# G's mixes by accumulating DMAs, w_out's mixes on VectorE, six batches' state products from one split of w_in, and the state read's scalings on ScalarE

## The chip, the cores and the metric

One core of a Trainium2 chip runs the whole program. The metric is device time in microseconds (us), the median of several executions; lower is better. Engines are named as in the profile: PE (TensorE), PEld (its weight loads), DVE (VectorE), ACT (ScalarE), POOL (GpSimd) and SP (SyncE, which issues most DMAs).

## What is computed

Attention between 512 tokens and 32 state rows per head, in both directions, and on its result a two-layer network with `h - tanh(h)` in the middle:

```python
scores = scale * np.matmul(x, state.transpose(0, 1, 3, 2))      # softmax over the 32 state rows
xread = np.matmul(a, state)
scores2 = scale * np.matmul(state, x.transpose(0, 1, 3, 2))     # softmax over the 512 tokens
sread = np.matmul(a2, x)
...
h = x @ w_in            # x: 4608 rows of 512 (8 batches of 512 + 32); w_in 512 x 2048
g = h - np.tanh(h)
return (g @ w_out)      # w_out 2048 x 512
```

## The kernel before

The 4096 token rows are eight chunks of 512, one for each batch; the 256 rows of the state read are a ninth, chunk 8. Since `xread` is `a @ state`, the kernel never forms it: for each batch it computes m = state x w_in (256 rows by 2048) and then h = a x m, in 16 *hidden tiles* of 128 columns (`Chunk.hidden`, L405 to L407; `finish` takes tanh on ACT and the difference on DVE, L419 and L421).

**Split products.** Each float32 operand is split into a high and a low part in the float32r format (`split`, L99: a cast on ACT, then a subtraction on DVE), and a product is three matmuls: high by high, high by low, low by high.

**Stage one** makes the chunks 0 and 1, while the weights come in as 64-bit words and are converted. w_in is kept in DRAM (`wf`), m of the batches 0 and 1 comes from whole-float32 matmuls (L165). m of the other six comes from generators, `m_units(g)`, of 16 units each, which split a piece of w_in (`wst`), multiply it by the state with 64-row matmuls (L198), copy out on ACT (L202), and store to DRAM (`mdram`, L205). g = 0 serves the batches 2 to 5. g = 1 serves 6 and 7: it reads and splits w_in a second time, has the state's high and low part side by side in one stationary operand, and leaves two addends, which `load_m` sums on DVE (L218). w_out's rows go to DRAM as high and low parts (`keep_row`, into `wod`), and `mix_rows` makes from each two rows four sums and differences of w_out's blocks (L718 to L723, on POOL), splits them and stores them in `wsd`.

**The pairs.** The chunks 2 to 7 are done as three pairs (`Pair`; the profile's W0m.., W1m.. and W2m.. tiles). With w_out in four blocks, a pair's product is made from seven block products instead of eight, m1 to m7 in the code, in the order of `ORDER`; some take mixes of the two chunks' g, some mixes of w_out. Each has four steps of twelve matmuls (L861), each step with a W tile of 512 KB loaded by SP (L807) into one of four `parts` buffers. The g of a pair stay whole in SBUF (`G`, in groups j = 0 to 3 of even and odd tiles, 128x1024 each). Mixes of G are made in place: two when four hidden tiles of the second chunk are done (`hidden_done`, L841), one ahead of each m5 split (L828), one behind each m6 split (L834), all on POOL but for six on DVE. A m5 product's operand is then split (`Pair.split`), and so on. While a pair runs its later products, the next chunk's hidden tiles stand between them. Chunk 8 comes last, with w_out's rows loaded back (`load_rows`).

**What sets the order.** A list of ticks, "P" for a product step and "H" for a hidden tile, is written out for each pair; tables (`ASIDE`, `KEEP`, `MIX`, `SIDES`) say at which step or tick a side unit (attention of a later batch, m units, rows kept, mixes) is handed over; the framework's scheduler then places instructions on each engine, which issues its own in that order. Pool sizes (`parts` 4, `twins` 2, two PSUM banks each in `ps_a` and `ps_h`) set when buffers come free.

**State read.** `state_read` divides by the softmax's sum with 64 scalings of 32x64 on DVE (L365).

Of the kernel before, what the change touches and what calls it, by code (L numbers as in the profile page):

```python
# [34 lines left out]
def attention_ffn(ctx: ExitStack, tc: tile.TileContext, xT, xn, bd, bh, sp, sm, sl, win, wout, xout, tout, sout):  # L35
# [133 lines left out]
    def m_units(g):  # L169

        raw = pool.tile([P, H, P], F32, tag="stage", name=f"smr{g}", bufs=SB)
        s = pool.tile([P, 2, H, P], F32R, tag="sm", name=f"sms{g}", bufs=1)
        if g == 0:
            nc.sync.dma_start(raw, sm)
            split(s[:, 0], s[:, 1], raw)
        else:
            nc.sync.dma_start(raw[:, :, 0:64], sl)  # L180
            split(s[:, 0, :, 0:64], s[:, 0, :, 64:128], raw[:, :, 0:64])
        for q in range(NQ):
            for k in range(2):
                w = pool.tile([P, 2, 512], F32, tag="wf", name=f"w1{g}{q}{k}", bufs=WB)
                nc.sync.dma_start(w, wf[q][:, 2 * k : 2 * k + 2])
                for c in range(2):
                    p = 2 * k + c

# [2 lines left out]
                    hs = slice(2 * c, 2 * c + 2)
                    stage = pool.tile([P, 2, 512], F32, tag="stage", name=f"st{g}{q}{p}", bufs=SB)
                    pss = [bank(ps_a, f"mps{g}{q}{2 * p + e}") for e in range(2)]
                    terms = [(0, 0), (0, 1)] + [(1, 0)] * (g == 0)
                    for n, (x, y) in enumerate(terms):
                        for e in range(2):
                            rows = slice(64 * e, 64 * e + 64)
                            nc.tensor.matmul(  # L198
                                pss[e], s[rows, x, 2 * p + e], t[rows, y], start=(n == 0), stop=(n == len(terms) - 1)
                            )  # L200
                    for e in range(2):
                        nc.scalar.copy(stage[:, e], pss[e])  # L202
                    for j in range(4):
                        dst = mdram[2 + j][q][0] if g == 0 else mdram[6 + j % 2][q][j // 2]
                        nc.sync.dma_start(dst[k, hs].rearrange("h n f -> n h f"), stage[32 * j : 32 * j + 32])  # L205
# [812 lines left out]
```

## Time and profile before

| | |
|---|---|
| median of 3 runs | 731.44 us (731.35 to 731.79) |
| the profiled execution | 733.29 us, its span 731.3 us |
| mean granted PE clock | 0.969 |
| busy PE, DVE, ACT, POOL | 670.3, 565.5, 399.3, 183.1 us |
| DMA | 164.29 MB, 225 GB/s on average |

The span reaches from the first to the last instruction of the profiled execution. Busy time of PE contains waits in its pipeline and slow clock, so that 92% is not all work. Rows of groups show line, engine, operation and tiles, then busy time and mean ns of one, then the idle time ahead of them and what ended it. In lists by time the first number is the start, the second the length.

### The profile page before, as it was taken

Reading aid. Unit: us, or ns where it says so; the run is one execution under the profiler, and the core shown is the slowest. Engines: PE = TensorE matmul, PEld = TensorE weight load, DVE = VectorE, ACT = ScalarE, POOL = GpSimd, SP = SyncE. Lnnn points to the kernel's source line nnn. Section 1 sums busy time; section 2 is a strip of 40 time slices with the busy share of each in tenths; the row PEclk is TensorE's granted clock in tenths of the full one; section 3 lists DMA queues with packets and bytes.
Section 4 is the critical chain, followed back from the end, with each engine's and each line's share of the span. In section 5 each row is a group of like instructions: output and inputs, shape, how many; then the busy total and the mean of one; then the engine's idle time right before and its main releaser. Section 6 shows DMA issues by size and latency. Waiting matters only on the chain.

```text
span 731.3 us, 9639 instructions
## 1 busy us (share of the span) xinstructions
PE 670.3 (92%) x3378; PEld 497.3 (68%) x3378; DVE 565.5 (77%) x781; ACT 399.3 (55%) x643; POOL 183.1 (25%) x99
## 2 busy tenths in 40 slices
PE   4899879999989798778999999788999999799997
PEld 2456657777766574556767777566788877587896
DVE  5899999769745979996669669997797698945442
ACT  3789757657545654535656666334654553343432
POOL 2000034755500025722000006563000069600000
PEclk9899999999999999998999999989999999999999
DMA  9799926986897545654788887647676644599600
GB/s 314 238 386 371 357 91 219 326 289 208 250 320 201 193 141 176 202 155 155 223 260 252 282 249 243 232 134 242 186 230 194 201 129 141 162 390 378 212 23 30
DMA packets 82672, 164.29 MB, mean 225 GB/s; under 512 B 8000, under 2 KB 40000, under 8 KB 82624
## 3 DMA queue, kind: packets, MB, share of 16 engines
q1 hardware_dynamic: 82624, 163.67, 67.5%
q8 instruction: 27, 0.44, 0.2%
q14 instruction: 21, 0.17, 0.1%
HBM read 116.98 MB, written 46.66 MB: 224 GB/s over the span
## 4 chain that ended last, share of the span: by engine, by line
PE 54%; DVE 28%; DMA 7%; issue 6%; ACT 2%; POOL 2%; SPq 0%; ACTq 0%; DVEq 0%; POOLq 0%
PE X L861 15%; PE hps L405 5%; PE hps L406 5%; PE hps L407 5%; PE Y0m L861 4%; DVE m L99 4%; PE mps L198 3%; PE Y1m L861 3%; PE ops L452 3%; PE ops L453 3%; PE ops L454 3%; DVE G L419 2%; PE Y2m L861 2%; POOL G L841 2%; DVE wst L99 1%
## 5 line engine op out<-in xcount | busy, mean ns | idle before, releaser
L841 POOL TENSOR_TENSOR G<-G,G 128x1024 f32<-128x1024 f32 x18 | 53.8, 2987 | 287.6 <-DVE G L419 286.9
L405 PE MATMUL hps<-aT,m 128*128 128x512 f32 x248 | 103.3, 417 | 18.4 <-DVE G L419 13.3
L406 PE MATMUL hps<-aT,m 128*128 128x512 f32 x248 | 99.7, 402 | 0.0
L407 PE MATMUL hps<-aT,m 128*128 128x512 f32 x248 | 99.4, 403 | 0.0
L419 DVE TENSOR_TENSOR G<-hps,t 128x512 f32<-128x512 f32 x96 | 64.9, 683 | 33.0 <-ACT t L419 32.7
L419 ACT ACTIVATE t<-hps 128x512 f32<-128x512 f32 x96 | 56.9, 597 | 57.1 <-PE hps L407 57.0
L405 PEld LDWEIGHTS hps<-aT,m 128*128 128x128 f32 x248 | 48.0, 194 | 41.9 <-DVE G L419 17.5
L99 DVE TENSOR_TENSOR g2m<-G,g2m 128x1024 fp32r<-128x1024 f32 x28 | 45.6, 1636 | 20.1 <-PE Y2m L861 7.8
L861 PE MATMUL X<-g0m,W0m 128*128 128x512 f32 x192 | 53.2, 421 | 6.5 <-ACT g0m L99 4.2
L407 PEld LDWEIGHTS hps<-aT,m 128*128 128x128 f32 x248 | 48.0, 194 | 12.0 <-issue 1.5
L406 PEld LDWEIGHTS hps<-aT,m 128*128 128x128 f32 x248 | 48.3, 195 | 11.0 <-issue 1.9
L453 PE MATMUL ops<-wo,g 128*128 128x512 f32 x128 | 51.3, 405 | 4.0 <-DVE wo L99 4.0
L718 POOL TENSOR_TENSOR wa<-wo 128x512 f32<-128x512 f32 x16 | 24.6, 1559 | 118.1 <-ACT wo11r L131 78.8
L99 ACT CAST g2m<-G 128x1024 fp32r<-128x1024 f32 x28 | 29.2, 1053 | 44.9 <-PE X L861 17.4
L99 DVE TENSOR_TENSOR m<-mr,m 128x1024 fp32r<-128x1024 f32 x31 | 51.2, 1653 | 1.3 <-ACT m L99 1.1
L861 PE MATMUL X<-g1m,W1m 128*128 128x512 f32 x192 | 50.0, 406 | 2.1 <-DVE g1m L99 2.1
L202 ACT COPY st<-mps 128x512 f32<-128x512 f32 x64 | 35.9, 589 | 29.3 <-PE mps L198 26.1
L861 PE MATMUL X<-g2m,W2m 128*128 128x512 f32 x192 | 47.1, 401 | 4.9 <-ACT g2m L99 2.8
L861 PEld LDWEIGHTS X<-g0m,W0m 128*128 128x128 f32 x192 | 37.2, 201 | 18.9 <-ACT g0m L99 4.8
L454 PE MATMUL ops<-wo,g 128*128 128x512 f32 x128 | 49.9, 395 | 0.0
L99 DVE TENSOR_TENSOR g1m<-G,g1m 128x1024 fp32r<-128x1024 f32 x28 | 39.5, 1416 | 12.4 <-PE X L861 7.3
L99 DVE TENSOR_TENSOR g0m<-G,g0m 128x1024 fp32r<-128x1024 f32 x28 | 38.2, 1366 | 12.2 <-ACT g0m L99 9.2
(265 smaller groups left out, 1465.8 us busy)
## 6 DMA issues: line engine op xcount, KB each, us to landing
md<-st SPq DMA_DIRECT2D x128, 128.0 KB, 2.6
mr<-md SPq DMA_DIRECT2D x24, 512.0 KB, 4.4
xT<-in_xT SPq DMA_DIRECT2D x16, 512.0 KB, 4.9
wod<-wo SPq DMA_DIRECT2D x16, 512.0 KB, 4.8
w<-wf SPq DMA_DIRECT2D x16, 512.0 KB, 4.4
wsd<-ws SPq DMA_DIRECT2D x16, 512.0 KB, 4.6
xn<-in_xn SPq DMA_DIRECT2D x16, 512.0 KB, 5.0
W0m<-wsd SPq DMA_DIRECT2D x16, 512.0 KB, 4.3
```

What stands on the lines that cost most here:

```text
L99: return nc.scalar.copy(hi, src), (sub or nc.vector).tensor_sub(lo, src, hi)
L198: nc.tensor.matmul(pss[e], s[rows, x, 2 * p + e], t[rows, y], start=(n == 0), stop=(n == len(terms) - 1))
L202: nc.scalar.copy(stage[:, e], pss[e])
L405: nc.tensor.matmul(ps, mhi[k][:, cols], ahi[:, k], start=(k == 0), stop=False)
L406: nc.tensor.matmul(ps, mhi[k][:, cols], alo[:, k], start=False, stop=False)
L407: made = nc.tensor.matmul(ps, mlo[k][:, cols], ahi[:, k], start=False, stop=(k == nk - 1))
L419: main(nc.scalar.activation(t, ps, AF.Tanh), nc.vector.tensor_sub(g, ps, t))
L453: nc.tensor.matmul(o, g[:, 0, tok], w[:, 1], start=False, stop=False)
L454: return nc.tensor.matmul(o, g[:, 1, tok], w[:, 0], start=False, stop=(f == NFF - 1)).ins
L718: nc.gpsimd.tensor_add(a[:, e].rearrange("p h n -> p (h n)"), w[:, 0], w[:, 1])
L841: main(eng.tensor_sub(c, d, c), eng.tensor_add(a, a, c))
L861: made = nc.tensor.matmul(out[t], w[:, e, x, cols], y[:, e], start=first and j == 0 and e == 0 and c == 0, stop=last and j == 3 and e == 1 ...
```

## The change

Four edits, and the tables that go with them.

1. G's mixes: `hidden_done` and both mixes in `split` become DMAs issued from POOL's queue that add their source onto their destination in SBUF (512 KB each, 48 in all). Since such a DMA only adds, half of the hidden tiles are stored with the other sign (t - h), m4's w_out block is stored negated, and some closing sums become differences. m5's mix now follows its split and m5 goes ahead of m6: m5 splits a, then a += d, then m6 splits a, then it is added onto m4's operand.
2. w_out's mixes: each converted row is also stored whole (`wfd`), `mix_rows` loads two rows from there, and makes the sums on DVE. m4's block, negated, is split and stored as a fifth row of `wsd`. `wod` is laid out by halves, so a row is stored and loaded back in two DMAs, and a pair's W tile is one run in a partition.
3. `m_units` has one generator: its 16 units serve all six batches. The batches 6 and 7 get 48 whole 128-row matmuls (one PSUM bank of `ps_h` a unit, `mls`) with a block-diagonal state operand, and one addend. The second pass (`m1` in the tables, 64 half-height matmuls, in the first two pairs) is gone, with its reads and splits of w_in and the sum in `load_m`.
4. The state read's 64 scalings are ACT activations with a scale.

```diff
-        "m0": [15, 16, 17, 17, 18, 19, 19, 20, 21, 21, 22, 23, 24, 25, 26, 27],
+        "m0": [14, 14, 15, 15, 16, 16, 17, 17, 18, 18, 19, 20, 20, 21, 22, 23],
...
-    MIX = [17 + 2 * x for x in range(7)] + [30]
+    MIX = [16, 17, 18, 19, 20, 22, 24, 26]
...
-            "m1": list(range(24, 72, 4)),
...
-            "m1": [2, 5, 8, 11],
...
+                    ps2 = bank(ps_h, f"mls{q}{p}")
...
+                    for n, (x, y) in enumerate(((0, 0), (0, 1), (1, 0))):
+                        nc.tensor.matmul(ps2, s1[:, x, p], t[:, y], start=(n == 0), stop=(n == 2))
+                    late = pool.tile([P, 512], F32, tag="c2", name=f"sl{q}{p}", bufs=CSB)
+                    nc.scalar.copy(late, ps2)
...
+                    for e in range(2):
+                        for j in range(2):
+                            rows = slice(64 * e + 32 * j, 64 * e + 32 * j + 32)
+                            nc.sync.dma_start(mdram[6 + j][q][k, 2 * c + e], late[rows])
...
-                nc.vector.tensor_add(r, r, r2)
...
+        nc.sync.dma_start(wfd[:, f], w)
...
-                nc.vector.tensor_scalar_mul(
+                nc.scalar.activation(
...
-                main(nc.scalar.activation(t, ps, AF.Tanh), nc.vector.tensor_sub(g, ps, t))
+                main(nc.scalar.activation(t, ps, AF.Tanh))
+                main(nc.vector.tensor_sub(g, ps, t) if f % 2 == i % 2 else nc.vector.tensor_sub(g, t, ps))
...
-        nc.sync.dma_start(wod[:, f % 2, f // 2], wo[f].bitcast(F32))
+        for half in range(2):
+            cols = slice(256 * half, 256 * half + 256)
+            nc.sync.dma_start(wod[:, f % 2, half, f // 2], wo[f][:, :, cols].bitcast(F32))
...
-        for e in range(2):
-            w = wo[2 * j + e].bitcast(F32)
-            nc.gpsimd.tensor_add(a[:, e].rearrange("p h n -> p (h n)"), w[:, 0], w[:, 1])
+        nc.sync.dma_start(a, wfd[:, 2 * j : 2 * j + 2].rearrange("p e (h n) -> p e h n", h=2))
...
+        nc.scalar.mul(neg[:, 0], a22, -1.0)
+        nc.vector.scalar_tensor_tensor(neg[:, 1], a22, -1.0, neg[:, 0], ALU.mult, ALU.subtract)
+        nc.sync.dma_start(wsd[:, 4, j // 2, j % 2], neg.bitcast(F32))
+        nc.vector.tensor_add(a22, a21, a22)
+        nc.vector.tensor_sub(a21, a11, a21)
+        nc.vector.tensor_sub(a11, a22, a11)
+        nc.vector.tensor_sub(a12, a11, a12)
...
-        ORDER = ("m1", "m2", "m6", "m5", "m7", "m3", "m4")
+        ORDER = ("m1", "m2", "m5", "m6", "m7", "m3", "m4")
...
-            if k == "m5":
-                main(nc.gpsimd.tensor_sub(src, self.source("m3", j), src))
...
+            if k == "m5":
+                main(self.add(src, self.source("m3", j)))
             if k == "m6":
-                b = self.source("m4", j)
-                main(nc.gpsimd.tensor_sub(b, b, src))
+                main(self.add(self.source("m4", j), src))
+
+        def add(self, dst, src):
+            return nc.gpsimd.dma_start(dst, src, accum_op=ALU.add)
...
-                eng = nc.vector if j == 3 else nc.gpsimd
-                main(eng.tensor_sub(c, d, c), eng.tensor_add(a, a, c))
+                main(self.add(a, c), self.add(c, d))
```

The instructions move with it. First PE in the first pair, before: `hps3_6` is a hidden tile of chunk 3, `mps100` an output of the second m pass, `sps41` scores of batch 4.

```order
L277 MATMUL sps41_2554<-xT40_2475,bdr4_2473 32x512 x2
L277 MATMUL sps41_2554<-xT41_2477,bdr4_2473 32x512 x2
L198 MATMUL mps100_2582<-wst100_2578,sms1_2572 128x512 x2
L405 MATMUL hps3_6_2626<-aT3_1840,m31_2491 128x512
L406 MATMUL hps3_6_2626<-aT3_1840,m31_2491 128x512
```

Now no such group stands in any pair. PE in stage one has the third output instead; these are the rows of one unit now (`mps20`, `mps21` the 64-row matmuls, `mls20` the whole ones), between a hidden tile of chunk 1 and its output product.

```order
L405 MATMUL hps1_4_1423<-aT1_517,m11_1420 128x512
L192 MATMUL mps20_1441<-wst20_1438,sms_1036 128x512
L192 MATMUL mps21_1442<-wst20_1438,sms_1036 128x512
L194 MATMUL mls20_1443<-wst20_1438,sls_1041 128x512
L192 MATMUL mps20_1441<-wst20_1438,sms_1036 128x512
L192 MATMUL mps21_1442<-wst20_1438,sms_1036 128x512
L192 MATMUL mps20_1441<-wst20_1438,sms_1036 128x512
L192 MATMUL mps21_1442<-wst20_1438,sms_1036 128x512
L194 MATMUL mls20_1443<-wst20_1438,sls_1041 128x512 x2
L451 MATMUL ops1_0_1303<-wo4_481,g1_4_1433 128x512
```

Each of the 16 units has gained three whole matmuls, and all of them now stand ahead of the first pair's first product; before, the last four 64-row outputs (12 matmuls) stood behind it. Last, POOL's queue in the third pair before: `G6` is the first chunk's g, `G7` the second's, the number behind them the first tile of the group.

```order
L841 TENSOR_TENSOR G7_4_5308<-G7_5_5319,G7_4_5308 128x1024 [waits DVE_49]
L841 TENSOR_TENSOR G6_4_4738<-G6_4_4738,G7_4_5308 128x1024 [waits Pool_49]
L834 TENSOR_TENSOR G6_5_4767<-G6_5_4767,G6_4_4738 128x1024 [waits Activation_49,Pool_49]
L828 TENSOR_TENSOR G6_0_4584<-G7_1_5231,G6_0_4584 128x1024 [waits DVE_49,Activation_49]
L841 TENSOR_TENSOR G7_8_5417<-G7_9_5428,G7_8_5417 128x1024 [waits DVE_49]
L841 TENSOR_TENSOR G6_8_4884<-G6_8_4884,G7_8_5417 128x1024 [waits Pool_49]
```

And now, with the semaphores that each waits for (DMASW are those of POOL's own DMAs):

```order
L838 DMA G6_0_4518<-G7_1_5153 128x1024 [waits DVE_49,Activation_49]
L838 DMA G6_8_4812<-G7_8_5333 128x1024 [waits DMASW7_49,DMASW5_49,DVE_49]
L838 DMA G6_1_4548<-G6_0_4518 128x1024 [waits DMASW4_49]
L838 DMA G7_8_5333<-G7_9_5344 128x1024 [waits DMASW5_49,DVE_49]
L838 DMA G6_4_4669<-G7_5_5238 128x1024 [waits DVE_49,Activation_49]
L838 DMA G6_8_4812<-G7_9_5344 128x1024 [waits DMASW1_49,DVE_49,Activation_49]
L838 DMA G6_12_5015<-G7_12_5418 128x1024 [waits DVE_49]
```

Each mix has become one DMA row; several wait for an earlier one's landing, and the group 12's first DMA stands behind the group 8's last.

More of the change, by code (lines that the diff above doesn't have):

```diff
@@ L187, in m_units @@
                     p = 2 * k + c
-                    t = twins(f"wst{g}{q}{p}", [P, 2, 512], F32R)
+                    t = twins(f"wst{q}{p}", [P, 2, 512], F32R)
                     split(t[:, 0], t[:, 1], w[:, c])
[L191 to L195, printed above, removed]
+                    pss = [bank(ps_a, f"mps{q}{2 * p + e}") for e in range(2)]
+                    ps2 = bank(ps_h, f"mls{q}{p}")
+                    for n, (x, y) in enumerate(((0, 0), (0, 1), (1, 0))):
                         for e in range(2):
                             rows = slice(64 * e, 64 * e + 64)
-                            nc.tensor.matmul(
-                                pss[e], s[rows, x, 2 * p + e], t[rows, y], start=(n == 0), stop=(n == len(terms) - 1)
-                            )
+                            nc.tensor.matmul(pss[e], s0[rows, x, 2 * p + e], t[rows, y], start=(n == 0), stop=(n == 2))
+                    for n, (x, y) in enumerate(((0, 0), (0, 1), (1, 0))):
+                        nc.tensor.matmul(ps2, s1[:, x, p], t[:, y], start=(n == 0), stop=(n == 2))
+                    late = pool.tile([P, 512], F32, tag="c2", name=f"sl{q}{p}", bufs=CSB)
+                    nc.scalar.copy(late, ps2)
+                    stage = pool.tile([P, 2, 512], F32, tag="stage", name=f"st{q}{p}", bufs=SB)
                     for e in range(2):
@@ L651, in attention_ffn @@
     first = afters[FILL[3]]
-    m1 = [m_units(g) for g in range(2)]
+    m1 = m_units()
     atts = {}
@@ L803, in load @@
                 odd, half = self.PURE[k]
-                src = wod[:, odd, 2 * j : 2 * j + 2, :, 256 * half : 256 * half + 256]
+                src = wod[:, odd, half, 2 * j : 2 * j + 2]
             else:
@@ L895, in load_rows @@
         wo[f] = big(f"wl{f}", [P, 2, DM], F32R)
-        nc.sync.dma_start(wo[f].bitcast(F32), wod[:, f % 2, f // 2])
+        for half in range(2):
+            cols = slice(256 * half, 256 * half + 256)
+            nc.sync.dma_start(wo[f][:, :, cols].bitcast(F32), wod[:, f % 2, half, f // 2])
     def hidden(c, f, own=None):
```

69 lines of the change are left out of this document (34 added, 35 removed).

## Prediction

> **What bounds the kernel now.** First the page, for the engines as a whole; then a table of engine busy time by stretch, to find where TensorE is not full.
>
> ```profile
> span 731.3 us, 9639 instructions
> PE 670.3 (92%) x3378; PEld 497.3 (68%) x3378; DVE 565.5 (77%) x781; ACT 399.3 (55%) x643; POOL 183.1 (25%) x99
> ...
> PE   4899879999989798778999999788999999799997
> ...
> POOL 2000034755500025722000006563000069600000
> PEclk9899999999999999998999999989999999999999
> DMA  9799926986897545654788887647676644599600
> ...
> PE 54%; DVE 28%; DMA 7%; issue 6%; ACT 2%; POOL 2%; SPq 0%; ACTq 0%; DVEq 0%; POOLq 0%
> ```
>
> PE is 92% busy, but its dips (slices 14 to 18, 25, 26 and 34) mostly sit where POOL is busy, and DVE holds 28% of the chain that ended last. So I cut the span at the first product of each of the three pairs (219.9, 423.0, 574.2) and at the last chunk (682.3).
>
> ```profile
> 0.00:219.91 219.91, 196.44 (x875) 135.63 (x875) 184.05 (x289) 143.25 (x249) 62.87 (x57) 0.98 0.82 280
> 219.91:423.00 203.09, 184.50 (x1025) 130.13 (x1025) 158.47 (x234) 113.76 (x181) 37.72 (x14) 0.96 0.65 203
> 423.00:574.20 151.20, 142.07 (x753) 108.12 (x752) 127.17 (x158) 77.12 (x113) 40.23 (x14) 0.95 0.67 216
> 574.20:682.30 108.10, 102.01 (x441) 82.59 (x441) 77.01 (x62) 46.34 (x59) 42.24 (x14) 0.98 0.69 242
> 682.30:731.30 49.00, 45.25 (x289) 40.81 (x287) 18.78 (x39) 18.82 (x44) 0.00 (x0) 0.98 0.17 56
> ```
>
> Columns: length, then PE, weight load, DVE, ACT and POOL busy, granted clock, DMA share, GB/s. Within the pairs, stretches without and with POOL work differ:
>
> ```profile
> 350.00:423.00 73.00, 73.00 (x433) 52.10 (x433) 51.21 (x89) 45.81 (x73) 0.00 (x0) 1.00 0.80 251
> 250.00:350.00 100.00, 82.86 (x435) 57.83 (x434) 86.26 (x108) 51.42 (x82) 37.72 (x14) 0.91 0.52 164
> 450.00:500.00 50.00, 40.87 (x217) 30.25 (x216) 49.45 (x54) 21.77 (x33) 27.86 (x11) 0.90 0.65 219
> 600.00:650.00 50.00, 45.01 (x189) 36.19 (x188) 39.91 (x28) 20.14 (x26) 33.33 (x11) 0.97 0.59 194
> ```
>
> Without POOL work PE is full at clock 1.00; with it, PE idles 17.1, 9.1 and 5.0 us and its clock falls as well. The reason is in DVE's own rows, grouped for 260 to 350 us (the first three lines) and for 350 to 410 us (the last two):
>
> ```profile
> L99 DVE TENSOR_TENSOR g0m<-G,g0m 128x1024 fp32r<-128x1024 f32 x12 | 18.6, 1558 | 6.0 <-ACT g0m L99 3.0 <-PE Y0m L861 1.5 <-issue 1.4
> L99 DVE TENSOR_TENSOR m<-mr,m 128x1024 fp32r<-128x1024 f32 x4 | 9.6, 2402 | 0.0
> L841 POOL TENSOR_TENSOR G<-G,G 128x1024 f32<-128x1024 f32 x6 | 16.8, 2793 | 86.0 <-DVE G L419 85.7
> ...
> L99 DVE TENSOR_TENSOR g0m<-G,g0m 128x1024 fp32r<-128x1024 f32 x11 | 13.4, 1221 | 5.1 <-ACT g0m L99 5.1
> L99 DVE TENSOR_TENSOR m<-mr,m 128x1024 fp32r<-128x1024 f32 x3 | 3.6, 1216 | 0.0
> ```
>
> The same subtraction takes 1.22 us alone and 1.56 to 2.40 us on average beside POOL's mixes: the two engines hold each other up, DVE falls behind, PE waits for it.
>
> **The change, part by part.** Names: a and c are the even tiles of a pair's first and second chunk, d the second's odd ones, with a number for the group of four.
>
> *G's mixes.* All 42 GpSimd subtractions and 6 on DVE become 48 accumulating DMAs, so DVE's operations go back to 1.22 us. The PE time to be had is idle time plus slow clock: 17.1 + (1 - 0.91) x 82.9 = 24.6 us in the first pair, 9.1 + 4.1 = 13.2 in the second, 5.0 + 1.4 = 6.4 in the third. If every operand then stood ready it would all come back. Against that stands the landing time t of an accumulating DMA, of which this trace has no row. The nearest are plain 512 KB DMAs:
>
> ```profile
> W0m<-wsd SPq DMA_DIRECT2D x16, 512.0 KB, 4.3
> W2m<-wsd SPq DMA_DIRECT2D x16, 512.0 KB, 5.0
> wo0d<-in_wout SPq DMA_DIRECT2D x1, 512.0 KB, 9.4
> 36.00:82.00 46.00, 44.38 (x174) 28.80 (x172) 44.35 (x80) 38.88 (x67) 0.00 (x0) 1.00 1.00 372
> ```
>
> Bounds: 4.3 us (a quiet queue) and 9.4 us (the slowest in the trace, in the start's saturated stretch). I take 6.5: the third pair's 5.0 plus a second 512 KB read at the 372 GB/s of a full stretch, 1.4 us. The Trainium skill bears on that second read: "Collectives: The Full Stack", Part 3, says that an add in the DMA path needs two source reads and so gets half a copy's rate. No run shows it yet; by a rate of half, 512 KB count as 1 MB.
>
> Four rows more, for what stands around such a DMA:
>
> ```profile
> L419 ACT ACTIVATE t<-hps 128x512 f32<-128x512 f32 x96 | 56.9, 597 | 57.1 <-PE hps L407 57.0
> L419 DVE TENSOR_TENSOR G<-hps,t 128x512 f32<-128x512 f32 x96 | 64.9, 683 | 33.0 <-ACT t L419 32.7
> L99 ACT CAST g2m<-G 128x1024 fp32r<-128x1024 f32 x28 | 29.2, 1053 | 44.9 <-PE X L861 17.4 <-PE Y2m L861 12.4 <-DVE G L841 8.3
> 522.93 2.72 PE X L861 x12
> ```
>
> What t costs: in the third pair the fourth m5 product is due 19.0 us after hidden tile 7_11 (five products of twelve matmuls, 2.72 us each, and four hidden tiles of six, 1.36). Its DMA (a12 += c12) can't be issued before tile 7_14 is through tanh and subtraction (0.60 + 0.68), 10.8 us after 7_11, and its operand then still has to be split, 2.3 us (ACT 1.05, DVE 1.22). Done at 10.8 + t + 2.3, it is late by t - 5.9. GpSimd's queue adds to it: a8 += c8, issued near 7_11, must land before a8's split, and the DMA a8 += d8, which waits for that split, stands ahead of a12's; above t = 8.5 the delay is therefore 2t + 4.6 - 19.0. Fourth m6 then needs t + 2.3 within four products, another t - 8.6. At 6.5 that is 0.6 us per pair. I keep 5, 4 and 3.4 us for this and for waits that stood behind the old ones: gains 20, 9 and 3.
>
> *w_in from one split.* PE's prices:
>
> ```profile
> 228.90 0.95 PE L198 MATMUL mps<-wst,sms 64*128 64x512 f32 x3
> 229.79 0.50 PE L405 MATMUL hps<-aT,m 128*128 128x512 f32 x1
> ...
> 290.05 0.73 PE L198 MATMUL mps<-wst,sms 64*128 64x512 f32 x2
> ...
> 290.71 0.50 PE L407 MATMUL hps<-aT,m 128*128 128x512 f32 x1
> ```
>
> A whole matmul costs 0.227 us (2.72 / 12), a lone group of two half-height ones 0.66 from start to start, of three 0.89. The 16 m1 units leave the pairs, about 1.2 us each: 12 in the first pair (14 us), 4 in the second (5). The last 12 half-height matmuls of m0, now before the first product instead of behind it, move 4 us from the first pair to stage one. Stage one also takes 48 new whole matmuls, 10.9 us, and about 1 us of extra switches: +16 there, -18 in the first pair, -5 in the second. Is stage one PE-bound where they land?
>
> ```profile
> 140.00:200.00 60.00, 60.00 (x285) 44.92 (x283) 46.85 (x66) 38.19 (x67) 34.74 (x30) 1.00 0.81 253
> ```
>
> PE is full from 140 to 200, so nothing hides them: the 16 us count whole. The floor would be nothing, if they filled the 23 us (219.9 - 196.4) that PE idles in stage one; but none of those lie here, where most of m0 falls.
>
> *DMA in stage one.*
>
> ```profile
> 197.97 6.99 DMA wsd<-ws
> ...
> 206.50 6.69 DMA out_x<-ob
> ...
> 422.44 0.43 SPq L205 DMA_DIRECT2D md<-st  x1
> ```
>
> New there: 16 w_out rows stored (4.2 MB), 8 loads of them (4.2), 8 negated blocks (2.1), 64 copies of late blocks (4.2): 14.7 MB. The share is 0.82 already (row above), at 280 GB/s; at 372 GB/s, 14.7 MB is 40 us of full load, and the room is 0.18 x 219.9 = 40 us. Between nothing and 40 I take 8 us: the start is saturated (1.00 above), and the stretch before the first product already waits for a store of mixes and one of outputs (first two rows), but the extra is spread out. SP issues all of it in order, about 110 issues more at 0.43 us, 47 us of SP's time in 220; a load of a w_out pair that waits for its buffer holds up m0's loads and stores and the first pair's weights behind it, and that is part of the 8.
>
> *Engines off the path.* Three rows price the rest.
>
> ```profile
> L365 DVE TENSOR_SCALAR sr<-rps,ri 32x64 f32<-32x64 f32 x64 | 18.0, 281 | 5.7 <-PE rps L359 4.7
> L218 DVE TENSOR_TENSOR mr<-mr,ml 128x1024 f32<-128x1024 f32 x8 | 15.9, 1992 | 4.1 <-DMA mr<-md 2.4 <-issue 1.0 <-DVE ri L342 0.7
> L99 DVE TENSOR_TENSOR wst<-w,wst 128x512 fp32r<-128x512 f32 x32 | 32.0, 1000 | 9.6 <-ACT wst L99 9.6
> ```
>
> DVE loses 18.0 + 15.9 + 16 us and gains 40 of 256 columns for w_out's mixes in stage one: between 0.28 us (64 columns, above) and 0.68 (512), say 0.4, 16 us; in return it no longer meets POOL's 62.9 us there. ACT takes the 64 scalings: from nothing more than DVE's 0.28 us each, 18 us, to twice that, on an engine that is idle 45% of the span; I count nothing. What hides them is that idle time; were it gone, tanh would come late and PE's hidden tiles with it. m0's third output takes the hidden tiles' two PSUM banks in turn; the first rival prices that.
>
> **Sum.** Stage one +16 + 8 = +24; first pair -20 - 18 = -38; second -9 - 5 = -14; third -3; last chunk 0. Total -31. Against the profiled run: its span 731.3 becomes 700.3, and 733.29 becomes 702.3. That run lies 1.85 us above the median of 731.44, so the median is forecast at 700.4, rounded 700.
>
> **Rivals.** *Stage one fills up.* All 40 us of new DMA load land on the path there instead of 8, or tanh waits for PSUM banks that m0's third output now shares. For it: share 0.82 to 1.00 above. Against: 100 us of it are PE-bound with DMA at 0.81. With 20 to 28 us more the time is 720 to 728. Chance 0.15.
>
> *Accumulating DMAs become the bound* (the other side). If t is long, each pair stalls at its fourth m5 and fourth m6 product by the two terms above: at 9.4 us 4.4 + 0.8 = 5.2 per pair, 16 in all, 714; at 11.5 us 8.6 + 2.9, 34 in all, and the gain is gone; at 15 us 15.6 + 6.4, 66 in all, 764. For it: pairs already run DMA at 0.65 to 0.69, and 48 DMAs add 25 MB of writes and up to 50 of reads against 17 MB taken away. Against: no 512 KB DMA of this trace lands later than 9.4. It decides at about 11.5 us. Chance 0.10.
>
> *The hold-up stays.* GpSimd still makes those DMAs' descriptors, and if DVE is held up by that as by the mixes, only the moved work is left: +24 - 18 - 5 = 732. For it: DVE slows beside every POOL mix seen here. Against: so far POOL read and wrote whole operands. Chance 0.05. The Trainium skill, "SBUF — State Buffer", section "Who interferes with whom", speaks against it: two-input subtractions would not meet descriptor writing; nothing here shows that.
>
> *Cover holds in stage one.* If DMA costs nothing, and part of the waits at 198 and 206 goes as m0 and the mixes now end earlier, stage one grows by 12 or so: 688. Chance 0.15.
>
> **How the numbers follow.** The forecast has 0.55; its own range, with stage one's DMA from 0 to 16 and t from 4.3 to 9.4, is 690 to 722. Rivals reach 682 below (688 with 6 us more from the kept waits) and 728 above; what lies outside is the third rival, most of the second and the forecast's tails, under 0.2. 0.2% of the time, 1.5 us, is about what a measurement of this kernel tells from no change. Faster: 0.55 + 0.15 + 0.15, less 0.01 for t near the deciding point: 0.84. Same: 0.03, slower: 0.13, shared between the second and third rivals and that 0.01.
>
> **What would show it.** Right: DVE's 128x1024 splits near 1.22 us throughout the pairs; no PE dip at 250 to 350; first product near 244 us; first pair near 165 us, second 137, third 105. Wrong: splits still at 1.6 or more, accumulating DMAs landing after 9 us, waits of g0m on them, or a first product past 255.

## The result, and the profile after

The changed kernel takes 755.87 us (median of 4 runs, 752.84 to 758.45) beside 731.62 us (731.35 to 732.8): a ratio of 1.0327, 95% interval [1.0283, 1.0371]. It is slower, on the other side of the forecast and outside its range. The profiled execution of one run below, e1, was in a slower state (823.79 us at a mean clock of 0.75, beside 715.81 to 719.83 us for its other three), so that only its time is used. First the page of the changed kernel.

```profile
span 756.7 us, 9651 instructions
PE 679.7 (90%) x3362; PEld 505.4 (67%) x3362; DVE 462.1 (61%) x727; ACT 405.4 (54%) x683; POOL 45.6 (6%) x57
...
PE   5899889986899888986899999789999998588997
...
POOL 1000000000000000121100001220000012100000
PEclk9899999998699999999999999988999999799999
DMA  9799988898888845799977678999656799999610
...
PE 40%; DMA 13%; DVE 1%; issue 1%; ACT 1%; POOL 0%; ACTq 0%; DVEq 0%; SPq 0%; POOLq 0%
```

DVE is down by 103 us of busy time and POOL by 137, and DVE's share of the chain that ended last has gone from 28% to 1%. DMA stands there now with 13%. The DMA row has nines in the slices 18 to 20, 26 to 28 and 33 to 37; before, of these only 36 and 37 had them. Next, the table by stretch: columns as before, cut at the first product of each pair (263.8, 442.4, 586.1) and at the last chunk (707.6).

```profile
0.00:263.80 263.80, 231.13 (x950) 152.89 (x951) 190.18 (x336) 164.21 (x291) 3.74 (x9) 0.94 0.90 300
263.80:442.40 178.60, 162.47 (x982) 122.83 (x982) 110.09 (x168) 100.62 (x175) 14.04 (x16) 0.96 0.76 214
442.40:586.10 143.70, 135.40 (x706) 105.42 (x705) 88.73 (x126) 75.76 (x117) 13.89 (x16) 0.95 0.83 228
586.10:707.60 121.50, 105.44 (x442) 83.51 (x441) 54.27 (x58) 46.06 (x59) 13.91 (x16) 0.94 0.98 283
707.60:756.70 49.10, 45.21 (x289) 40.77 (x287) 18.78 (x39) 18.78 (x44) 0.00 (x0) 1.00 0.17 56
```

Stage one grew by 43.9 us. The first pair shrank by 24.5 and the second by 7.5, and the third, the shortest, grew by 13.4. Its DMA share is 0.98. Now the groups of the splits of the three pairs, and POOL's DMA issues.

```profile
L838 POOL DMA_DIRECT2D G<-G x48 | 41.8, 884 | 610.2 <-DVE ri L340 295.0 <-DVE G L418 107.6 <-DMA G<-G 76.8
...
L100 DVE TENSOR_TENSOR g0m<-G,g0m 128x1024 fp32r<-128x1024 f32 x28 | 34.0, 1221 | 23.7 <-ACT g0m L100 18.6 <-PE X L864 3.2 <-PE Y0m L864 1.8
L100 DVE TENSOR_TENSOR g1m<-G,g1m 128x1024 fp32r<-128x1024 f32 x28 | 33.9, 1220 | 20.1 <-ACT g1m L100 11.6 <-PE X L864 5.6 <-ACT s1m L880 2.1
L100 DVE TENSOR_TENSOR g2m<-G,g2m 128x1024 fp32r<-128x1024 f32 x28 | 33.9, 1223 | 45.2 <-ACT g2m L100 20.8 <-PE X L864 12.6 <-issue 5.7
```

The splits take 1.22 us in all three pairs: the hold-up of DVE is gone, as forecast, and descriptor writing on POOL does not bring it back. What came in its place is in the page's rows of DMAs (queue with packets, MB and its share of 16 engines; then KB each and median us to landing):

```profile
q0 software_dynamic: 6912, 25.17, 17.6%
...
G<-G POOLq DMA_DIRECT2D x48, 512.0 KB, 9.3
...
W2m<-wsd SPq DMA_DIRECT2D x20, 512.0 KB, 7.8
```

An accumulating DMA lands after 9.3 us, not 6.5, and 17.6% of 756.7 us is 133 us of all 16 engines for 48 of them, 2.77 us each. The third pair's weights land after 7.8 us, where they took 5.0. In the list of waits (total, times, longest) these stand:

```profile
POOL G L838 <- DMA G<-G: 76.8, 17, 11.2
...
ACT g2m L100 <- DMA G<-G: 20.4, 2, 13.8
...
ACT wn L719 <- DMA wa<-wfd: 18.4, 6, 5.7
ACT g1m L100 <- DMA G<-G: 16.5, 3, 7.4
```

The timeline of ACT and PE in the second pair shows how such a wait reaches PE (start, length, in brackets the idle time before and its releaser):

```profile
488.52 1.04 ACT L100 CAST g1m<-G 128x1024 fp32r<-128x1024 f32 x1 [7.39 <-DMA G<-G]
489.48 1.08 ACT L417 ACTIVATE t<-hps 128x512 f32<-128x512 f32 x2
...
490.84 0.80 PE L403 MATMUL hps<-aT,m 128*128 128x512 f32 x1 [4.61 <-DVE G L418]
```

ACT's cast waits 7.4 us for a landing, and two tanh stand behind it in ACT's queue. PE, whose hidden tile needs the PSUM bank that they free, idles 4.6 us, and the wait is put down to DVE's subtraction behind the tanh. In the third pair PE's longest wait, 7.9 us at the fourth m5 product, is for a cast that waits for the addition issued at 638.58. From there to 696.4 us the chain is mostly transfers: the five pieces below are 45.7 of these 57.8 us (first the row of waits, then start and length).

```profile
PE Y2m L864 <- ACT g2m L100: 7.9, 1, 7.9
...
638.58 11.29 DMA G<-G
...
653.36 10.37 DMA wl<-wod
663.80 9.82 DMA W2m<-wsd
676.50 7.00 DMA W2m<-wsd
689.11 7.25 DMA W2m<-wsd
```

Last, stage one. The stretch from 180 to 200 us, in which PE was full before, and two lines of it:

```profile
180.00:200.00 20.00, 12.76 (x36) 6.81 (x34) 14.28 (x28) 9.34 (x18) 0.00 (x0) 0.66 0.95 315
```

```profile
186.15 0.42 ACT L719 ACTIVATE wn<-wa 128x256 fp32r<-128x256 f32 x1 [5.66 <-DMA wa<-wfd]
...
187.12 0.79 PE L192 MATMUL mps<-wst,sms 64*128 64x512 f32 x2 [4.50 <-ACT wst L100]
```

ACT waits for a pair of w_out's rows, with the cast of w_in's piece behind it, and PE waits for that cast. The granted clock is 0.66 in this stretch.

### The profile page after: what moved, and what is told of

It reads as the page before. It is cut to its first block, busy times and chain, and to the rows that moved or that the text cites. A ratio compares the mean times of both kernels' runs of the same rounds, so it can differ in the third digit from the quotient of the medians.

```text
span 756.7 us, 9651 instructions
## 1 busy us (share of the span) xinstructions
PE 679.7 (90%) x3362; PEld 505.4 (67%) x3362; DVE 462.1 (61%) x727; ACT 405.4 (54%) x683; POOL 45.6 (6%) x57
## 3 DMA queue, kind: packets, MB, share of 16 engines
q0 software_dynamic: 6912, 25.17, 17.6%
## 4 chain that ended last, share of the span: by engine, by line
PE 40%; DMA 13%; DVE 1%; issue 1%; ACT 1%; POOL 0%; ACTq 0%; DVEq 0%; SPq 0%; POOLq 0%
PE X L864 14%; DMA G<-G 5%; PE hps L403 5%; PE hps L404 5%; PE hps L405 5%; DMA W2m<-wsd 3%; PE Y1m L864 3%; DMA W1m<-wsd 2%; PE Y2m L864 2%; PE Y0m L864 2%; DMA out_t<-ob0m 2%; DMA wl<-wod 1%; PE ops L452 1%; PE ops L451 1%; PE ops L453 1%
## 5 line engine op out<-in xcount | busy, mean ns | idle before, releaser
L838 POOL DMA_DIRECT2D G<-G x48 | 41.8, 884 | 610.2 <-DVE ri L340 295.0
L100 DVE TENSOR_TENSOR g2m<-G,g2m 128x1024 fp32r<-128x1024 f32 x28 | 33.9, 1223 | 45.2 <-ACT g2m L100 20.8
L418 DVE TENSOR_TENSOR G<-t,hps 128x512 f32<-128x512 f32 x48 | 32.7, 682 | 45.6 <-ACT t L417 45.6
L452 PE MATMUL ops<-wo,g 128*128 128x512 f32 x128 | 53.0, 414 | 3.1 <-DVE wo L100 3.0
L864 PE MATMUL X<-g0m,W0m 128*128 128x512 f32 x192 | 51.0, 407 | 4.6 <-DVE g0m L100 2.3
L418 DVE TENSOR_TENSOR G<-hps,t 128x512 f32<-128x512 f32 x48 | 33.0, 687 | 33.5 <-ACT t L417 33.2
L451 PE MATMUL ops<-wo,g 128*128 128x512 f32 x128 | 46.7, 421 | 5.4 <-ACT g L100 3.4
L100 ACT CAST g1m<-G 128x1024 fp32r<-128x1024 f32 x28 | 29.1, 1052 | 36.7 <-DMA G<-G 16.5
L100 DVE TENSOR_TENSOR g0m<-G,g0m 128x1024 fp32r<-128x1024 f32 x28 | 34.0, 1221 | 23.7 <-ACT g0m L100 18.6
L453 PE MATMUL ops<-wo,g 128*128 128x512 f32 x128 | 47.7, 405 | 0.0
L864 PE MATMUL X<-g1m,W1m 128*128 128x512 f32 x192 | 46.8, 391 | 1.0 <-DMA W1m<-wsd 1.0
L100 DVE TENSOR_TENSOR g1m<-G,g1m 128x1024 fp32r<-128x1024 f32 x28 | 33.9, 1220 | 20.1 <-ACT g1m L100 11.6
```

Source lines behind the costliest of these rows:

```text
L100: return nc.scalar.copy(hi, src), (sub or nc.vector).tensor_sub(lo, src, hi)
L418: main(nc.vector.tensor_sub(g, ps, t) if f % 2 == i % 2 else nc.vector.tensor_sub(g, t, ps))
L451: nc.tensor.matmul(o, g[:, 0, tok], w[:, 0], start=(f == 0), stop=False)
L452: nc.tensor.matmul(o, g[:, 0, tok], w[:, 1], start=False, stop=False)
L453: return nc.tensor.matmul(o, g[:, 1, tok], w[:, 0], start=False, stop=(f == NFF - 1)).ins
L838: return nc.gpsimd.dma_start(dst, src, accum_op=ALU.add)
```

## The experiments

Two questions: is the loss in the pairs that of the accumulating DMAs, and by what mechanism, and what fills stage one? The stretches of every run that is read below, in us from its timeline, cut at the first m0 matmul (m units of the batches 2 to 5) and then as above. Each row is one profiled execution, which lies up to 4.3 us from the run's median (f1 4.3 above it, e4 4.2 below), so a difference of a few us between two rows is not firm.

| run | to first m0 | to first product | pair 1 | pair 2 | pair 3 | median |
|---|---|---|---|---|---|---|
| before | 105.9 | 114.0 | 203.1 | 151.2 | 108.1 | 731.62 |
| after | 109.1 | 154.7 | 178.5 | 143.7 | 121.5 | 755.87 |
| e2_g_mixes_pool | 108.9 | 152.1 | 173.8 | 138.8 | 111.4 | 735.6 |
| e3_wout_resident | 101.6 | 154.1 | 177.2 | 142.7 | 120.4 | 745.81 |
| e4_both | 101.7 | 151.9 | 167.9 | 133.2 | 101.7 | 711.45 |
| e5_plain_copy | 109.4 | 151.8 | 171.8 | 129.6 | 105.8 | 716.43 |
| f1_two_pass_m | 104.7 | 128.3 | 182.1 | 142.3 | 101.8 | 705.56 |
| f2_m0_spread | 102.7 | 143.5 | 171.1 | 133.2 | 101.3 | 702.36 |
| f3_neg_buffer | 102.4 | 148.3 | 170.4 | 133.2 | 100.8 | 705.73 |
| g1_spread_and_buffer | 102.7 | 140.3 | 170.4 | 133.2 | 102.0 | 698.34 |
| g2_before_g_dve | 106.0 | 113.7 | 192.9 | 146.2 | 101.0 | 710.57 |
| g3_before_g_dve_one_split | 106.8 | 131.1 | 174.3 | 136.4 | 100.0 | 702.54 |
| g4_rows_late | 108.0 | 152.5 | 178.1 | 143.5 | 120.2 | 753.82 |
| h1_dma_where_slack | 104.3 | 138.2 | 165.1 | 132.7 | 107.4 | 698.92 |
| h3_dma_where_due | 101.7 | 140.0 | 172.4 | 135.3 | 110.9 | 710.63 |
| j1_dma_queue_order | 103.2 | 138.3 | 180.3 | 145.2 | 125.6 | 744.07 |
| j2_dma_all | 102.7 | 138.0 | 177.5 | 141.8 | 120.3 | 733.6 |

**e1, G's mixes on DVE.** The changed kernel with one line exchanged:

```diff
         def add(self, dst, src):
-            return nc.gpsimd.dma_start(dst, src, accum_op=ALU.add)
+            return nc.vector.tensor_add(dst, dst, src)
```

> The changed kernel with G's 48 mixes as additions on VectorE in place of accumulating DMAs; all else stays. Theory: the DMAs' landing (9.3 us, median) is what stalls the pairs and fills the DMA engines in the third; so the three pairs (178.6, 143.7, 121.5 us) fall to about 160, 135 and 106, stage one stays at 264, and the time is about 714. Rival 1 (VectorE becomes the bound: 48 additions of 1.26 us are 60 us more on an engine that also makes the splits): the pairs stay as they are or lengthen, 750 or more. Rival 2 (the loss is all in stage one, the pairs are held by something else): the time stays within 5 us of 756.

718.05 us, ratio to before 0.9808 [0.9774, 0.9841], near the 714 of its theory and 38 us less than the changed kernel. The accumulating DMAs alone turn a gain into a loss.

**e2, the same additions on POOL** (`nc.gpsimd.tensor_add(dst, dst, src)`).

> The changed kernel with G's 48 mixes as additions on GpSimd, as the kernel before had them, with the new order m5 ahead of m6. Theory: the hold-up between GpSimd and VectorE comes back, VectorE's 128x1024 splits beside it go from 1.22 us to 1.6 to 2.4, and the pairs take what they took before less the second m pass: about 183, 147 and 107 us; with stage one at 264 the time is about 750. Rival (the hold-up never cost much, the landing time of the DMAs is the whole loss): as with VectorE, about 714.

735.6, ratio 1.0059 [1.0038, 1.0081], lower than expected. The hold-up comes back, with the splits of the three pairs at 1.45, 1.66 and 1.74 us on average; but even so POOL is cheaper here than the DMAs, by 20 us, half of it in the third pair (111.4 beside 121.5).

**e3, w_out's sums made from the rows in SBUF**, without `wfd`.

```diff
-        nc.sync.dma_start(wfd[:, f], w)
...
-        nc.sync.dma_start(a, wfd[:, 2 * j : 2 * j + 2].rearrange("p e (h n) -> p e h n", h=2))
+        for e in range(2):
+            w = wo[2 * j + e].bitcast(F32)
+            nc.vector.tensor_add(a[:, e].rearrange("p h n -> p (h n)"), w[:, 0], w[:, 1])
```

> The changed kernel with the w_out mixes' inputs made on VectorE from the rows that are in SBUF (high plus low part), instead of being stored to DRAM and loaded back; no row is stored whole. Theory: ScalarE's wait for those loads (18.4 us in six waits, with the splits for m0 queued behind it) is what stage one loses beyond its new matmuls; stage one goes from 264 to about 245, the time to about 738. Rival (stage one is long because of the new matmuls and of DMA load as a whole, 0.90 share): it shortens by less than 6 us, since 8.4 of 79 MB go, and the time stays at 750 or above.

745.81, ratio 1.0192 [1.0169, 1.0215]. This lies between what its theory and its rival gave. In stage one the gain is all ahead of the first m0 matmul (109.1 to 101.6), where `wfd` was stored; from there to the first product nothing changed (154.7 and 154.1). Taking away ACT's wait for these loads, which the timeline shows so plainly, thus did not shorten that part, and the reading that it is what stage one loses fell. Another wait of ACT stands there now, for the store of the negated block:

```profile
ACT wst L100 <- DMA wsd<-wn: 8.3, 3, 3.4
```

**e4, e1 and e3 together.**

> Both edits at once: G's mixes on VectorE and the w_out mixes from the rows in SBUF. Theory: the gains add up, 714 less 18, about 697. Rival (one loss stands behind the other, or VectorE is full): 715 or more.

711.45, ratio 0.9716 [0.9683, 0.9749]. The gains of e1 and e3, 37.8 and 10.1 us, nearly add up; the 697 of its theory was missed because e3 brought 10 us and not 18. Its pairs take 167.9, 133.2 and 101.7 us, close to or under the forecast's 165, 137 and 105. What is left above the forecast is stage one.

**e5, DMAs that copy where they added** (`nc.gpsimd.dma_start(dst, src)`), same queue, same order, same waits; the additions are left out.

> The changed kernel with the 48 accumulating DMAs as plain copies of the same tiles from the same queue: the additions are left out, everything that waits for them still waits. Theory A (the second read of the destination makes them land late, so the engines' share of 17.6% for 25 MB falls to about half): landing falls from 9.3 to about 5 to 6 us, the third pair from 121.5 to about 108. Theory B (they land late because GpSimd makes the descriptors, or because the engines are full with other transfers): landing stays at 8 us or more, the third pair at 118 or more.

716.43 (2 runs), ratio 0.978 [0.9719, 0.9841]. The page, and the third pair in the table by stretch:

```profile
q0 software_dynamic: 6912, 25.17, 8.7%
...
G<-G POOLq DMA_DIRECT2D x48, 512.0 KB, 6.2
```

```profile
562.60:668.40 105.80, 100.82 (x441) 81.13 (x440) 54.53 (x58) 46.20 (x59) 8.46 (x16) 1.00 0.91 323
```

The same bytes in the same packets take 8.7% of 717.5 us, 62 us of all engines or 1.30 each instead of 2.77, and land after 6.2 us, close to the 6.5 that the forecast took. The pairs are 36.5 us shorter. So the loss is neither the issuing on POOL nor the order, but the cost of the addition in the DMA engines.

**f1, m of the batches 6 and 7 by a second pass, as before**, on e4.

```diff
-    m1 = m_units()
+    m1 = [m_units(g) for g in range(2)]
...
-        "m0": [14, 14, 15, 15, 16, 16, 17, 17, 18, 18, 19, 20, 20, 21, 22, 23],
+        "m0": [15, 16, 17, 17, 18, 19, 19, 20, 21, 21, 22, 23, 24, 25, 26, 27],
...
+            "m1": list(range(24, 72, 4)),
```

> The kernel with both edits (G's mixes and w_out's on VectorE, from SBUF) with the state products of the batches 6 and 7 again from a second pass over w_in in the first two pairs. Theory (the single split costs stage one more than it saves the pairs): from the first m0 matmul to the first pair's product 152 falls to about 118, the first two pairs lengthen by 16 and 5, and the time goes from 711 to about 695. Rival (stage one is long for another reason, VectorE's w_out mixes or DMA load): stage one stays above 140 and the time rises to 720 or more.

**f2, only that table of m0's places, on e4.**

> The kernel with both edits, with m0's 16 units handed over at the steps of the kernel before (15 to 27) instead of 14 to 23. Theory (two units a step crowd ScalarE, which then keeps PE waiting; PE's idle time and slow clock of some 15 us in stage one come from that): stage one 253.6 falls by 5 to 10, the time to about 703. Rival (it is the matmuls and their switches alone): within 3 us of 711.

**f3, only the negated block's buffer, on e4**: from the pool that w_in's splits share to another.

```diff
-        hl = pool.tile([P, 2, 2, 256], F32R, tag="twins", name=f"wn{j}")
-        neg = hl[:, 0]
+        neg = pool.tile([P, 2, 256], F32R, tag="c2", name=f"wn{j}", bufs=CSB)
```

> The kernel with both edits, with the negated w_out block split into another buffer, so that it no longer shares two buffers with the split of w_in that m0 reads. Theory (7.5 us of ScalarE's waits in stage one are for that block's store to DRAM to free the buffer, with m0's matmuls behind): stage one falls by about 4 us, the time to about 707. Rival (other waits take its place): within 2 us of 711.

**g1, f2 and f3 together.**

> The kernel with G's and w_out's mixes on VectorE (w_out's from SBUF), m0 spread over the steps 15 to 27, and the negated block in a buffer of its own kind. Theory (crowding and the shared buffer are two separate waits of ScalarE in stage one): stage one falls by 4 more than with the spread alone, the time to about 698. Rival (they are the same wait, seen twice): 702.

f1 705.56, ratio 0.9643 [0.9603, 0.9683]; f2 702.36, 0.9593 [0.9559, 0.9627]; f3 705.73, 0.9638 [0.9606, 0.967]; g1 698.34, 0.9552 [0.9513, 0.9591]. f2, f3 and g1 came as expected. Between first m0 and first product, f2 to e4 shows what the table's crowding costs, 8.4 us (143.5 to 151.9), and g1 to f2 the shared buffer, 3.2 (140.3 to 143.5). f1 missed by 10, and it does not price the single split cleanly: f1 to f2 is 15.2 us there (128.3 to 143.5) and 11.0, 9.1 and 0.5 in the pairs, but in f1 the first product waits 5.48 us for its W tile, which it does in no other of these runs:

```profile
232.96 3.35 PE L872 MATMUL X<-g0m,W0m 128*128 128x512 f32 x7 [5.48 <-DMA W0m<-wod]
```

Nor are f1's 14.3 us over the kernel before (128.3 and 114.0) all due to w_out's new mixes: besides that wait, 28 matmuls stand ahead of the first product in f1 that stood behind it before, m0's last 12 (4 us by the prediction) and 16 of the scores (about 1 us in the kernel before). g2 and g3 below are the cleaner pair. g1 is the fastest version of all, and the table by stretch shows its pairs, without those DMAs:

```profile
242.90:413.30 170.40, 160.46 (x982) 122.00 (x981) 126.23 (x185) 101.86 (x176) 0.00 (x0) 0.97 0.53 175
413.30:546.50 133.20, 131.55 (x705) 102.63 (x704) 106.23 (x142) 76.44 (x117) 0.00 (x0) 1.00 0.56 182
546.50:648.50 102.00, 100.23 (x442) 81.32 (x441) 71.52 (x74) 46.69 (x59) 0.00 (x0) 1.00 0.75 255
```

PE is nearly full from the second pair on (131.6 of 133.2 us, 100.2 of 102.0) at clock 1.00. The third pair leaves 0.25 x 102.0 = 25.5 us of DMA time free; the first leaves 80.

**g2, the kernel before with its G mixes on DVE** (the four `nc.gpsimd` of its G mixes become `nc.vector`), **and g3, the same with one split of w_in** (f1's edit the other way round, with the table of before).

> The kernel before with one part alone: all of G's 48 mixes as additions and subtractions on VectorE, none on GpSimd. Theory (the hold-up between GpSimd and VectorE was the whole loss in the pairs, and the rest of the change costs stage one more than it brings): stage one stays at 220, the pairs are those of the two-pass kernel, 182, 142 and 102, last chunk 49, so 695 in the span and about 696. Rival (the w_out mixes on VectorE are needed too, since GpSimd's own hold VectorE up in stage one): over 705, with a longer stage one.

> The same with the single split of w_in for six batches added, its units at the steps 15 to 27 as before; w_out's mixes stay on GpSimd. Theory (the 48 new matmuls cost stage one about 16 and the second pass cost the pairs about 20): stage one 236, pairs 171, 133 and 102, the time about 692. Rival (GpSimd's mixes, the state operand's buffer and m0 crowd stage one together): stage one 245 or more, 700 or more.

710.57, ratio 0.9722 [0.9686, 0.9758], and 702.54, 0.9612 [0.9577, 0.9648]. Without POOL's mixes the pairs give back 10.2, 5.0 and 7.1 us, 22 in all; g2 is 15 above what was expected, most of it in the first pair, 192.9 instead of 182: the 182 came from f1, and by the estimate above about 5 of the 11 us are the 28 matmuls that f1 has ahead of that pair. One split then takes 18.6, 9.8 and 1.0 us off the pairs and puts 18.2 into stage one (237.9 less 219.7, where 236 was expected); g3's time is 10 above its theory, as g2's pairs were too long already.

**g4, chunk 8's rows loaded later**, to see whether they crowd the third pair.

```diff
-            if n == 2 and at >= len(ticks) - 14 and nrow < NFF:
+            if n == 2 and at >= len(ticks) and nrow < NFF:
```

> The changed kernel with w_out's rows loaded back only behind the third pair instead of during its last 14 ticks. Theory (in the third pair the accumulating DMAs take room from these loads and the W tiles, so that DMA is full at 0.98): the third pair falls from 121.5 to about 110, and the last chunk lengthens since its rows come later. Rival (the third pair is held by the landing of its mixes alone): it stays above 118.

753.82 (2 runs), ratio 1.0322 [1.0272, 1.0372]. It decides nothing: the scheduler issued the loads during the third pair all the same (648.9 to 697.4 us).

**h1 and h3, half of the additions as DMAs, on g1.** h1 takes the 24 whose result is needed late (c += d, and m4's operand), h3 the 24 that a split waits for soon (a += c, a += d); the rest stay on DVE. In h1:

```diff
-                main(self.add(self.source("m4", j), src))
+                main(self.add(self.source("m4", j), src, True))
...
+            if late:
+                return nc.gpsimd.dma_start(dst, src, accum_op=ALU.add)
...
-                main(self.add(a, c), self.add(c, d))
+                main(self.add(a, c), self.add(c, d, True))
```

> The spread-and-buffer kernel (698) with 24 of the 48 mixes as accumulating DMAs again: c += d (due 16 products later) and m6's operand onto m4's (due 12 products later); the two that make m5's and m6's operands stay on VectorE. Theory (due time): the pairs stay within 3 us each of 170, 133 and 102, the time within 4 of 698, since nothing waits for these within their landing. Rival (DMA load): the third pair lengthens by 5 or more, as W tiles and rows come later, and the time goes to 705 or more.

> The complement: the 24 mixes a += c and a += d, which make m5's and m6's operands, as accumulating DMAs, the other 24 on VectorE. Theory (due time): most of the loss returns, the pairs lengthen by 6 to 15 us each, the time is 720 or more. Rival (DMA load): the same as the other half, within 5 us of that run.

698.92, ratio 0.9539 [0.95, 0.9578], and 710.63, 0.9704 [0.9668, 0.974]. Where the result is due late, 24 DMAs cost nothing in sum, as h1's theory had it, though the third pair lengthens as its rival said; where it is due soon, 12 us, less than the 22 or more of h3's theory. Against g1 the first two pairs win 5.8 us in h1 and lose 4.1 in h3; the third loses in both, 5.4 and 8.9. Its stretch and the landing, first h1, then h3:

```profile
540.30:647.70 107.40, 102.47 (x441) 83.73 (x440) 63.35 (x66) 46.84 (x59) 6.96 (x8) 0.97 0.91 282
```

```profile
G<-G POOLq DMA_DIRECT2D x24, 512.0 KB, 7.9
```

```profile
549.40:660.30 110.90, 101.94 (x441) 82.31 (x440) 63.54 (x66) 46.31 (x59) 6.97 (x8) 0.97 0.89 272
```

```profile
G<-G POOLq DMA_DIRECT2D x24, 512.0 KB, 6.0
```

**j1 and j2: the order of POOL's queue, or the load?** Nothing and 12 us for the halves, some 34 to 41 for the whole: either additions due soon stand in POOL's queue behind c += d, which waits for a landing, or the load itself does it. j2 is g1 with all 48 as DMAs; j1 also moves each c += d behind m5's addition:

```diff
             if k == "m5":
-                main(self.add(src, self.source("m3", j)))
+                x = self.add(src, self.source("m3", j))
+                with tc.issue_after(x.ins):
+                    y = self.add(self.source("m7", j), self.source("m3", j))
+                main(x, y)
```

> All 48 additions as accumulating DMAs on the best version (698), but each c += d stands behind m5's a += d in GpSimd's queue, so that no addition that is due soon waits behind one that waits for a landing. If the surplus over the 24 that are due soon (710.6) is the order of the queue, about 712, and GpSimd's own waits for G's DMAs go well below 77 us. If it is the load of the DMA engines, as slow as with the old order: 730 to 740.

> All 48 additions as accumulating DMAs on the best version, in the changed kernel's order. The additions cost 34 (with the old stage one and w_out's mixes aside) to 41 us in the pairs of the other versions, so 698 + 34 to 41 = 732 to 739 by both theories; under 725, and the surplus would be that of a fuller stage one and not of the queue or the load.

j2 733.6, ratio 1.0033 [1.001, 1.0057], as expected: 35 us over g1, with stage one within 2.3 us of g1's. j1 744.07, ratio 1.0179 [1.0134, 1.0224], over what either theory gave. POOL's wait for its own DMAs and the third pair in j2, then that wait in j1:

```profile
POOL G L838 <- DMA G<-G: 74.8, 17, 10.9
```

```profile
560.00:680.30 120.30, 104.94 (x442) 83.33 (x441) 54.37 (x58) 46.05 (x59) 13.92 (x16) 0.96 0.97 285
```

```profile
POOL G L841 <- DMA G<-G: 35.1, 8, 9.5
```

The waits in POOL's queue are halved and the kernel is 10 us slower: the queue's order was not the cause, and that theory falls. Why j1 is slower than j2 stays open; its DMAs land after 10.1 us, j2's after 9.7.

The load explains the third pair by a sum. g1 uses 0.75 x 102.0 = 76.5 us of DMA time there; sixteen additions (the x16 under POOL) at 2.77 us add 44.3, together 120.8 us, and j2 takes 120.3 at a share of 0.97: sixteen don't fit into the old length, in whatever order. With sixteen copies the sum is 76.5 + 16 x 1.30 = 97.3, and e5 shows 0.91 x 105.8 = 96.3. With eight additions it is 98.7, and h1 and h3 show 97.7 and 98.7; these would fit into 102 us on the mean. PE's waits there are 4.9 us for W tiles in h1, and 5.7 us at the fourth m5 product for its operand in h3.

The first two pairs seem to have room, with a mean DMA share of 0.74 and 0.81 in j2, but the mean hides where the additions stand. Most of a pair's sixteen are issued in one part of it, from the third m2 product to the first m6 product. The next rows are that part in the three pairs, first in g1, then in j2 (a packet counts where it starts, so that a short stretch can show a share over 1):

```profile
297.30:336.80 39.50, 33.18 (x190) 25.87 (x190) 38.13 (x53) 19.60 (x34) 0.00 (x0) 0.91 0.48 160
448.40:476.30 27.90, 26.25 (x174) 19.65 (x173) 27.90 (x38) 16.36 (x29) 0.00 (x0) 1.00 0.56 190
580.00:602.90 22.90, 22.08 (x97) 17.94 (x96) 22.90 (x25) 10.29 (x13) 0.00 (x0) 1.00 0.55 188
```

```profile
294.90:342.00 47.10, 34.34 (x194) 26.18 (x193) 27.96 (x46) 20.68 (x37) 11.30 (x13) 0.89 1.04 260
453.20:490.80 37.60, 29.31 (x177) 21.66 (x176) 16.80 (x26) 16.38 (x29) 8.75 (x11) 0.86 1.04 260
593.50:629.30 35.80, 26.09 (x97) 20.20 (x96) 12.94 (x15) 10.05 (x13) 8.73 (x11) 0.86 1.04 256
```

These parts are 7.6, 9.7 and 12.9 us longer in j2, 30 of the 34 us that its pairs lose, and DMA is full in all three. Eleven to thirteen additions at 2.77 us need 30 to 36 us of DMA time, where g1 leaves 10 to 21. e5's copies, in the same places and order, take 36.7, 25.4 and 22.1 us there at a share of 0.91 to 0.98: no loss. This is why the whole costs more than its halves, +15.7 us in the first two pairs against -5.8 and +4.1 for h1 and h3, whose shares there are 0.94 to 0.98 and 0.89 to 0.97.

The landing shows the same. The first four additions of j2's third pair (issued from 571 to 590 us, one at a time) and nine in the crowd of its second (459 to 489 us):

```profile
G<-G POOLq DMA_DIRECT2D x4, 512.0 KB, 4.8
```

```profile
G<-G POOLq DMA_DIRECT2D x9, 512.0 KB, 10.5
```

## Why the prediction was wrong

The account of the change, in profiled spans: stage one +43.9, the pairs -59.6 without the DMAs (462.4 before, 402.8 in e4), +40.9 by the DMAs (443.7), the last chunk +0.2: 731.3 becomes 756.7. The forecast had +24 and -55. (The +40.9 is on the high side: e4 also leaves `wfd` out, and its profiled execution lies 4.2 us below its median, that of the changed kernel 2.6 above. From e3 to e4, which differ in the additions alone, it is 37.5 in the pairs and 34.4 between medians.)

*The hold-up on DVE: right.* The splits run at 1.22 us, and with the additions on DVE the pairs take what was forecast (402.8 in e4; 407 forecast); with them on POOL the splits slow down again (1.45 to 1.74 us in e2). The Trainium skill, "SBUF — State Buffer", section "Who interferes with whom", by which two-input subtractions don't meet descriptor writing, agrees with the splits' 1.22 us beside 48 DMAs issued by POOL. The gain by itself, before to g2, is 22 us where the forecast had 32.

*What an accumulating DMA costs: the step that failed.* The prediction gives all of them one landing time: "I take 6.5: the third pair's 5.0 plus a second 512 KB read at the 372 GB/s of a full stretch, 1.4 us." With it the pairs were to lose 5, 4 and 3.4 us to such waits and others, 12.4 in all; the additions cost 37.5 (e3 to e4). The landing is no single number: 4.8 us for additions issued one at a time and 10.5 in the crowd (j2), 9.3 in the median of the changed kernel, almost the upper bound of 9.4, which came from the saturated stretch at the start.

The place was right. In j2's pairs PE waits for the fourth m5 product's operand for 4.1, 5.5 and 7.2 us, where the formula gives 5.0 at 9.7 us, and for the fourth m6's for 2.5 us in the third pair alone, where it gives 1.1. But in all the formula gives 2 x 9.7 + 4.6 - 19.0 + 1.1 = 6.1 us a pair, 18 for the three, and j2 loses 7.1, 8.6 and 18.3. It has no place for hidden tiles held up behind a cast that waits (2.7 and 2.5 us in the second and third pair), for W tiles that come late (3.1 us in the third), or for the clock, 0.86 to 0.89 in the crowded parts beside 0.91 to 1.00 in g1.

*The term that was missing: the transfers' own time.* The formula knows only the landing of one DMA, and not that many additions in a short time fill the DMA engines and so lengthen that landing. Rows of the prediction were enough to see it in the third pair: 0.69 x 108.1 = 74.6 us of DMA there, and sixteen times 1 MB at 372 GB/s another 45, makes 120 us where 105 were forecast. The megabytes stood under the second rival ("25 MB of writes and up to 50 of reads"), but were never set against the room of one stretch. The Trainium skill's rule for an add in the DMA path ("Collectives: The Full Stack", Part 3) had the price: half a copy's rate. The runs agree, with 2.77 us against 1.30, 0.47 of the rate; the forecast put that rule into a latency and not into the load.

*The second rival had the sign.* It decides "at about 11.5 us", where the gain would be gone; it was gone at 9.3. Stage one's unforeseen 20 us are not the reason alone: 756.7 less 20 is 736.7, still above 731.3. The rival, too, counted latency only.

*w_in from one split: right as a trade.* Forecast +16, -18 and -5; g2 to g3, which differ in it alone, show +18.2, -18.6 and -9.8.

*Stage one: too low by 20 us.* First m0 is 3.2 us later. Between it and the first product 40.7 us were added. Runs that follow each other edit by edit divide them so: before to g2 -0.3; g2 to g3, the single split, 17.4; g3 to g1, w_out's new mixes on DVE, the negated block and the changed order of attention units, 9.2 (of which g1's earlier first m0 takes 4.1 back); g1 to f2, the shared buffer, 3.2; f2 to e4, the crowded table, 8.4; e4 to the changed kernel 2.8. The forecast had nothing for the 9.2, as DVE was thought free enough, for the 3.2 and for the 8.4. The 9.2 are not taken apart further, and each of these numbers carries the few us by which single executions differ. The 8 us for DMA had about the right size but another place: `wfd`'s stores cost 7.5 us ahead of the first m0 (e3). That the forecast priced each piece of work and not the table that packs it is why "filled up" was given 0.15, and only with DMA or PSUM banks as its cause.

## What to carry to other kernels

Before moving arithmetic into transfers, add up the DMA time of the part of the kernel in which they will be issued (share times length, plus the new transfers at their rate, twice the bytes for an addition) and see whether it still fits. Take that part, and not the kernel or a whole stage: j2's second pair shows a share of 0.81 in the mean, and 1.04 in the 38 us that hold eleven of its sixteen additions. The latency of one transfer is not its price: here it was 4.8 us alone and 10.5 in the crowd. And when a table is written anew together with an edit, the table has a price of its own: here the old spacing alone gave back 9 of 711 us.
